# One transfer for the four leftover row blocks of w1, issued earlier, with a new written-out order of all engines

## The chip, the cores and the metric

The kernel runs on one core of a Trainium2 chip. The core has a matmul engine (PE, whose weight loads the profile lists as PEld), a vector engine (DVE), an activation engine (ACT), a small general engine (POOL), a queue engine that mostly issues transfers (SP), and 16 DMA engines that carry them. The metric is the device time of one execution in microseconds (us); lower is better. Three runs of the kernel before gave a median of 148.53 us, 147.5 to 148.92.

## What is computed

The input is a sequence `x` of 2048 rows of 448 numbers. It is normalised row by row, and the normalised rows go two ways: through a diagonal complex recurrence over the sequence (a state-space model), and through a two-layer perceptron with a second normalisation ahead of it. The second result, passed through silu, gates the first.

```python
x = A_x                                   # [1, 2048, 448]
xn = _layernorm(x)
# A: the recurrence; Lam_bar, B_bar from Lambda, log_dt, B; y = 2 Re(C h) + xn * Dskip
h_t = Lam_bar * h_(t-1) + (xn_t @ B_bar.T)
s = 2.0 * real(hs @ C.T) + xn * Dskip
# B: the perceptron, F = 1792
y = _layernorm(xn)
g = silu(gelu(y @ w1 + b1) @ w2 + b2)     # w1 [448, 1792], w2 [1792, 448]
return x + s * g
```

## The kernel before

The sequence is worked in four groups (g = 0 to 3) of 512 positions. For each group the kernel does the first perceptron layer (`mm1_phase`, matmuls on line L661, gelu on ACT at L667 into `gT`), the second layer (`mm2`, L783 and L786, silu at L789 into `g_sb`), the input side of the recurrence (`bu_phase`, L690 into PSUM, copied to `u_sb` and `ue` by `copy` at L301 on ACT or L302 on DVE), the scan itself on DVE (`ssm`: products at L739 to L743, two scans at L749, products at L763 to L768 that make `hx` and `hz`), and the output side (`yt`, L805, L806, L813, L814 on PE, then L826 and L828 on DVE). Matmuls of neighbouring groups are interleaved, so PE changes between the perceptron and the recurrence many times.

The first group is special. Its first layer starts before all of `x` and `w1` has come, so it is done in halves: the first 256 positions (b = 0) for fi = 0 to 11, then fi = 12 and 13 for both halves at 512 columns, then the second 256 positions (b = 1). The names in the code for the transposed normalised rows are `xmT0p0` and `xmT0p1` (first half, transposed on PE) and `xmT1p0`, `xmT1p1` (second half: four DVE instructions at L401 write `xn2_sb`, then a DMA transpose at L77 issued by SP writes `xn2T`).

`w1` has 448 rows, that is three blocks of 128 and a remainder of 64. It is loaded in four parts by columns, of 256, 512, 512 and 512 columns (`CH`, parts 0 to 3). Each part is a transfer of the three full blocks (`w1_c`), a transfer of the remaining 64 rows (`w1r_c`), and a copy on the core of 64 rows into the other half of the partitions (`w1c_c`). A matmul of a part waits for that part's `w1_c` and `w1r_c`, and the second half of each accumulation also for `w1c_c`.

Work is recorded as numbered tasks with the names they read and write. The order in which the tasks are issued is the list `ORDER`, one sequence from which every engine takes its own tasks in turn; `SECOND` lists the tasks that take their second choice of engine (a copy, for example, has ACT first and DVE second). Each engine therefore works in a fixed order, waits where a task needs a name that has not been written yet, and holds everything behind it meanwhile. `D` (the skip weights) and `b2` are one row of 448 each (`dbr0`, `dbr1`), turned into columns by five tiny matmuls on PE (`skip_columns`, L554 and L555) and copied to `db` on DVE.

Of the kernel before, what the change touches and what calls it, by code (L numbers as in the profile page):

```python
# [148 lines left out]
def dram_ap(t, offset, ap):  # L149
    return bass.AP(tensor=t.tensor, offset=offset, ap=ap)  # L150
# [1 line left out]


ORDER = [int(k) for k in """
# [18 lines left out]
""".split()]  # L173
SECOND = [int(k) for k in """
26 29 48 49 59 61 65 69 74 75 76 77 87 89 90 91 113 115 172 178 204 205 206 208 209 210 212 214 216 218 220 222 234 236 238 240 242 244 248 250 252
256 270 277 322 324 336 339 350 352 360 365 399 409 429 443 444 445 446 472 473 475 487 488 528 529 530 542 549 561 575
""".split()]


# [18 lines left out]
def bass_recurrent_scan__ssm_conv_s5__mixer_channel_mlp__prompt_kernel(  # L198
# [11 lines left out]
    L, D, F = 2048, 448, 1792  # L210
# [6 lines left out]
    with ExitStack() as es:  # L217
        def SB(name, shape, dtype=BF):
            return es.enter_context(nc.sbuf_tensor(name, shape, dtype))
# [12 lines left out]
        w1_sb = SB("w1_sb", [128, 4, F])  # L232
# [61 lines left out]
        def act(fn, reads=(), writes=()):  # L294
            kb.add("act", fn, reads, writes)

        def pe(fn, reads=(), writes=(), split=False):
            kb.add("pe", fn, reads, writes, split=split)

        def copy(pairs, rd, wr):  # L300
            kb.either(("act", [lambda e, o=o, i=i: e.activation(o, i, ACT.Copy) for o, i in pairs]),  # L301
                      ("dve", [lambda e, o=o, i=i: e.tensor_copy(o, i) for o, i in pairs]), rd, wr)  # L302

        with nc.Block():  # L304
# [17 lines left out]
            def ld(eng, o, i, writes, reads=()):  # L322
                kb.dma(eng, o, i, reads=reads, writes=writes)
# [4 lines left out]
            def ldx(b0, n, reads=()):  # L328
                ld("sp", x_all[:, b0:b0 + n, :, :], dram_ap(A_x, b0 * 256 * D, [[2 * D, 128], [256 * D, n], [D, 2], [1, D]]),
                   [f"x{b}" for b in range(b0, b0 + n)], reads)  # L330
# [4 lines left out]
            def ldw1(c):  # L335
                a, w = CH[c][0] * 128, CH[c][1] * 128
                ld("sp", w1_sb[:, 0:3, a:a + w], dram_ap(B_w1, a, [[F, 128], [128 * F, 3], [1, w]]), [f"w1_{c}"])
                ld("sp", w1_sb[64:128, 3, a:a + w], dram_ap(B_w1, 384 * F + a, [[F, 64], [1, w]]), [f"w1r_{c}"])
                copy([(w1_sb[0:64, 3, a:a + w], w1_sb[64:128, 2, a:a + w])], [f"w1_{c}"], [f"w1c_{c}"])

            for par in range(2):
                ld("sp", x_all[:, 0, par, :], dram_ap(A_x, par * D, [[2 * D, 128], [1, D]]), [f"x0p{par}"])
            ldx(1, 1)
            ldw1(0)
            ld("act", brows[0:3, :], dram_ap(B_b1, 256, [[512, 3], [1, 512]]), ["br0"], ["br"])
            ld("act", brows[3:4, 0:256], dram_ap(B_b1, 0, [[256, 1], [1, 256]]), ["br1"], ["br"])
            for c in range(1, 4):
                ldw1(c)
# [291 lines left out]
            def fcol(fi):  # L640
                a, n = CH[chunk[fi]]
                return slice(a * 128 + fi - a, (a + n) * 128, n)
# [3 lines left out]
            def wg(g):  # L646
                return f"Wg{g}"

            def mm1_phase(g, b, j, pair, second):
                gx = gb = g % 2  # L650
                cols = slice(0, 512) if b is None else slice(b * 256, (b + 1) * 256)
                rhs = xn2T[:, gx, :, :, :].rearrange("p b (r d) c -> p d (b r) c", r=2) if b is None else xn2T[:, gx, b, :, :].rearrange("p (r d) c -> p d r c", r=2)
                xk2 = [f"xmT{gx}"] if g else ["xmT0p0", "xmT0p1"][:2 * (b != 1)] + ["xmT1p0", "xmT1p1"][:2 * (b != 0)] + ["xmT0"]
                c, bk = chunk[2 * j], MB[pair]

                def dst(bank):
                    return psum[:, bank, cols].rearrange("p (q c) -> p q c", c=128)

                def one_mm(k, n, h):
                    rows, d = slice(64 * h, 64 * h + 64), (0, 1, 2 + h, 3 - h)[n]  # L660
                    return lambda e: e.matmul(dst(bk[k]), w1_sb[rows, d, fcol(2 * j + k)], rhs[rows, d], start=not second and n == 0, stop=second and n == 3)  # L661
                pe([one_mm(h if not second else 1 - h, n, h) for n in range(4 if second else 3) for h in (0, 1)],
                   xk2 + [f"w1_{c}", f"w1r_{c}"] + ([f"w1c_{c}"] if second else []), [f"ps{bk[0]}", f"ps{bk[1]}"], split=True)
                if second:
                    for k in range(2):
                        fi = 2 * j + k
                        act(lambda e, k=k, fi=fi: e.activation(gT[:, gb, fi, cols], psum[:, bk[k], cols], ACT.Gelu_apprx_tanh,  # L667
                                                               bias=b1f[:, fi:fi + 1]),
                            ["b1f", f"ps{bk[k]}", wg(g)], [f"gT{gb}_{fi}_{q}" for q in ((0, 1) if b is None else (b,))])

            def mm1_run(g, b, js, pairs):
                for j in js:
                    mm1_phase(g, b, j, pairs[j - js[0]], False)
                    if j > js[0]:
                        mm1_phase(g, b, j - 1, pairs[j - 1 - js[0]], True)
                mm1_phase(g, b, js[-1], pairs[js[-1] - js[0]], True)
# [294 lines left out]
```

## Time and profile before

| | |
|---|---|
| median of three runs | 148.53 us (147.5 to 148.92) |
| the profiled execution | 148.91 us |
| span of its instructions | 147.2 us |
| what lies around the span | 1.71 us |
| granted PE clock | 0.997 |
| busy | PE 138.9, DVE 129.1, ACT 102.5, POOL 26.0 us |

Busy time of an engine is the time in which it had an instruction under way, and the chain of the profile is followed back from the last instruction, at each step to what released it. In the time lines, the number in brackets behind a row is how long the engine stood idle before it and what released it. `w_sb` stands for `w1_sb` and `w2_sb` alike, `xn_sb` for `xn_sb` and `xn2_sb`, `dk` for the little buffer that first holds the parameter rows, `vs` and `s_w` for the scan's input and output.

### The profile page before, as it was taken

What the parts mean: (1) busy time and instruction counts of PE and PEld (TensorE: products, weight loads), DVE (VectorE), ACT (ScalarE), POOL (GpSimd) and SP (SyncE); (2) the same over time, 40 slices, a digit from 0 to 9 for tenths busy, and PEclk for the clock granted to TensorE, in tenths of its full rate; (3) what the DMA queues carried; (4) which work ended last, traced back from release to release, by engine and by line L of the source; (5) the groups of instructions that cost most, each with busy time, mean ns of one, the idle gap of its engine ahead of it and who ended that gap; (6) DMA issues with size and microseconds to landing.
All of it is one profiled execution on the core that took longest, in us unless ns stands there. A gap on an engine that the chain in (4) does not pass through costs nothing.

```text
span 147.2 us, 3611 instructions
## 1 busy us (share of the span) xinstructions
PE 138.9 (94%) x1454; PEld 92.1 (63%) x1460; DVE 129.1 (88%) x281; ACT 102.5 (70%) x185; POOL 26.0 (18%) x79
## 2 busy tenths in 40 slices
PE   7993999999999999999999999999999999999990
PEld 7882774454455486566758545887766668564870
DVE  2899799999997399999999999596899999999891
ACT  3695899988789986879999931836686996064100
POOL 3484450000960000007600000002000700000000
PEclk9999999999999999999999999999999999999998
DMA  4899992988989946000000627517440011105114
GB/s 111 241 241 130 399 372 74 198 186 114 213 158 165 181 94 130 4 0 2 4 0 0 114 51 143 107 22 141 89 151 0 4 62 62 21 1 107 68 57 125
DMA packets 38850, 15.98 MB, mean 109 GB/s; under 512 B 33193, under 2 KB 38450, under 8 KB 38834
## 3 DMA queue, kind: packets, MB, share of 16 engines
q1 hardware_dynamic: 38276, 15.52, 47.8%
q10 hardware_dynamic: 558, 0.24, 0.6%
q8 instruction: 11, 0.18, 0.5%
q14 instruction: 5, 0.04, 0.1%
HBM read 5.86 MB, written 1.84 MB: 52 GB/s over the span
## 4 chain that ended last, share of the span: by engine, by line
PE 84%; DMA 4%; SPq 4%; DVE 3%; issue 1%; DVEq 0%
PE psum L661 27%; PE psum L783 24%; PE psum L690 15%; PE psum L805 6%; PE psum L806 5%; PE psum L786 4%; DMA w_sb<-in_B_w_dram 4%; SPq L78 4%; PE psum L813 2%; DVE t L828 2%; DVE tmp L826 1%; DVE Bn L861 1%; PE psum L814 0%; DVEq L304 0%; DVEq L131 0%
## 5 line engine op out<-in xcount | busy, mean ns | idle before, releaser
L661 PE MATMUL psum<-xn2T,w_sb 64*128 64x512 bf16 (+1 forms) x476 | 46.9, 340 | 2.6 <-DMA w_sb<-in_B_w_dram 2.3
L667 ACT ACTIVATE gT<-psum,b1f 128x512 bf16<-128x512 f32 (+1 forms) x68 | 37.5, 615 | 6.4 <-PE psum L661 6.1
L783 PE MATMUL psum<-gT,w_sb 128*128 128x512 bf16 x162 | 36.1, 379 | 0.6 <-issue 0.5
L661 PEld LDWEIGHTS psum<-xn2T,w_sb 64*128 64x128 bf16 x476 | 25.2, 109 | 17.9 <-DMA w_sb<-in_B_w_dram 2.5
L783 PEld LDWEIGHTS psum<-gT,w_sb 128*128 128x128 bf16 x168 | 16.2, 98 | 19.1 <-issue 0.4
L690 PE MATMUL psum<-xnT,BT 64*128 64x256 bf16 x392 | 24.6, 270 | 0.0
L690 PEld LDWEIGHTS psum<-xnT,BT 64*128 64x128 bf16 x392 | 18.9, 94 | 6.3 <-issue 0.8
L789 ACT ACTIVATE g_sb<-psum,db 128x512 bf16<-128x512 f32 (+1 forms) x16 | 9.6, 627 | 10.7 <-PE psum L783 8.1
L749 DVE TENSOR_TENSOR_SCAN s_w<-vs,dk 128x786 f32<-128x786 bf16 (+1 forms) x8 | 16.3, 2054 | 0.0
L826 DVE SCALAR_TENSOR_TENSOR tmp<-xnT,db,psum 128x512 f32<-128x512 bf16 (+1 forms) x17 | 10.9, 652 | 2.7 <-PE psum L806 2.2
L301 ACT ACTIVATE vs<-s_w 64x258 bf16<-64x258 f32 (+2 forms) x12 | 8.1, 688 | 6.5 <-DVE s_w L749 6.4
L443 ACT ACTIVATE xn_sb<-x_all,lnw 128x384 bf16<-128x384 bf16 (+2 forms) x18 | 11.0, 649 | 1.0 <-DVE xn_sb L442 0.9
L805 PE MATMUL psum<-hx,CZ 128*128 128x256 bf16 x84 | 10.8, 276 | 0.0
L465 ACT ACT_TABLE_LOAD x8 | 10.3, 1283 | 0.4
L806 PE MATMUL psum<-Bn,CQ 128*128 128x256 bf16 x84 | 10.5, 272 | 0.0
L805 PEld LDWEIGHTS psum<-hx,CZ 128*128 128x128 bf16 x84 | 7.9, 98 | 2.3 <-issue 0.8
L806 PEld LDWEIGHTS psum<-Bn,CQ 128*128 128x128 bf16 x84 | 8.2, 98 | 1.2
L828 DVE TENSOR_TENSOR t<-tmp,g_sb 128x512 bf16<-128x512 f32 (+1 forms) x14 | 8.5, 628 | 0.1
L364 DVE BATCH_NORM_STATS2 lnst<-x_all 128x6 f32<-128x448 bf16 x12 | 7.3, 619 | 0.9 <-DMA x_all<-in_A_x_dram 0.9
L422 POOL TENSOR_SCALAR lnw<-lnmv 128x4 f32<-128x4 f32 x3 | 0.7, 233 | 38.7 <-DVE lnmv L368 38.6
L301 ACT ACTIVATE u_sb<-psum 128x256 bf16<-128x256 f32 (+1 forms) x12 | 5.4, 489 | 2.8 <-PE psum L690 2.8
L761 POOL CAST vs<-cur 128x8 bf16<-128x8 f32 x3 | 2.5, 830 | 26.9 <-DVE cur L759 26.8
(155 smaller groups left out, 190.9 us busy)
## 6 DMA issues: line engine op xcount, KB each, us to landing
x_all<-in_A_x_dram SPq DMA_DIRECT2D x3, 448.0 KB, 6.2
w_sb<-in_B_w_dram SPq DMA_DIRECT2D x3, 448.0 KB, 6.8
out_dram<-Bn SPq DMA_DIRECT2D x6, 224.0 KB, 2.1
w_sb<-in_B_w_dram SPq DMA_DIRECT2D x3, 384.0 KB, 3.9
Bn<-in_A_B_re_dram SPq DMA_DIRECT2D x1, 336.0 KB, 8.1
Bn<-in_A_B_im_dram SPq DMA_DIRECT2D x1, 336.0 KB, 8.5
x_all<-in_A_x_dram SPq DMA_DIRECT2D x2, 112.0 KB, 2.1
x_all<-in_A_x_dram SPq DMA_DIRECT2D x1, 224.0 KB, 2.6
```

The lines of the kernel that those rows point to most:

```text
L301: kb.either(("act", [lambda e, o=o, i=i: e.activation(o, i, ACT.Copy) for o, i in pairs]), ("dve", [lambda e, o=o, i=i: e.tensor_copy(o, i ...
L443: ("act", [lambda e, o=o, i=i: e.activation(o, i, ACT.Identity, bias=nb, scale=rs) for o, i in parts]),
L465: kb.add("act", lambda e: e.preload_act_table_set(what), reads, writes, sem=name)
L661: return lambda e: e.matmul(dst(bk[k]), w1_sb[rows, d, fcol(2 * j + k)], rhs[rows, d], start=not second and n == 0, stop=second and n == 3)
L667: act(lambda e, k=k, fi=fi: e.activation(gT[:, gb, fi, cols], psum[:, bk[k], cols], ACT.Gelu_apprx_tanh, bias=b1f[:, fi:fi + 1]), ["b1f", ...
L690: fns.append(lambda e, rows=rows, bank=bank, m=m, o=o, n=n: e.matmul(psum[:, bank, c * NK:(c + 1) * NK].rearrange("p (b c) -> p b c", b=2) ...
L749: dve(lambda e, so=so, vi=vi, di=di: e.tensor_tensor_scan(so, vi, di, 0.0, ALU.add, ALU.mult), ["v", "vl", "vz", "dk", "dk01"] + ["v3"] * ...
L783: pe([lambda e, fi=fi: e.matmul(psum[:, bk, :], w2_sb[:, fi, 128 * j:128 * j + 128], gT[:, gb, fi, :], start=fi == 0, stop=fi == NF - 1) f ...
L805: pe([lambda e, k=k: e.matmul(par(psum[:, bk, :], 1), CZ[:, k, cols], halves(hx[:, hb, k, 1:NK + 1]), start=k == 0, stop=k == 6) for k in ...
L806: fns = [lambda e, k=k: e.matmul(par(psum[:, bk, :], 0), CQ[:, k, cols], halves(hz[:, hb, k, :]), start=not by_pe and k == 0, stop=not by_ ...
L826: dve([lambda e, o=o, p=p, x=x, d=d: e.scalar_tensor_tensor(out=v(o), in0=x, scalar=d, in1=v(p), op0=ALU.mult, op1=ALU.add) for o, p, x, d ...
L828: dve(lambda e: e.tensor_tensor(t3[:, 512 * j:512 * j + n], s, g_sb[:, hb, 512 * j:512 * j + n], ALU.mult), [ks, f"g{hb}_{j}"], [f"t3{j}"])
```

## The change

The four transfers of the remaining 64 rows become one transfer of all 1792 columns (`w1r`), recorded ahead of part 0 and issued by SP behind the first of the four parts in its order. The row transfers for `D` and `b2` are issued behind the last part of `w1`. Every matmul of the first layer now waits for the one name `w1r`. The copy `w1c_c` still waits for `w1_c`.

```diff
             def ldw1(c):
                 a, w = CH[c][0] * 128, CH[c][1] * 128
                 ld("sp", w1_sb[:, 0:3, a:a + w], dram_ap(B_w1, a, [[F, 128], [128 * F, 3], [1, w]]), [f"w1_{c}"])
-                ld("sp", w1_sb[64:128, 3, a:a + w], dram_ap(B_w1, 384 * F + a, [[F, 64], [1, w]]), [f"w1r_{c}"])
                 copy([(w1_sb[0:64, 3, a:a + w], w1_sb[64:128, 2, a:a + w])], [f"w1_{c}"], [f"w1c_{c}"])
...
             ldx(1, 1)
+            ld("sp", w1_sb[64:128, 3, :], dram_ap(B_w1, 384 * F, [[F, 64], [1, F]]), ["w1r"])
             ldw1(0)
...
-                   xk2 + [f"w1_{c}", f"w1r_{c}"] + ([f"w1c_{c}"] if second else []), [f"ps{bk[0]}", f"ps{bk[1]}"], split=True)
+                   xk2 + [f"w1_{c}", "w1r"] + ([f"w1c_{c}"] if second else []), [f"ps{bk[0]}", f"ps{bk[1]}"], split=True)
...
 ORDER = [int(k) for k in """
-2 3 16 17 14 15 11 9 13 4 44 0 1 22 18 5 24 25 19 20 93 23 94 12 95 45 92 46 42 105 47 96 97 106 49 50 101 107 98 111 110 99 102 48 51 52 100 103 41
+11 12 41 14 15 13 16 17 4 10 18 9 0 1 42 22 89 90 357 91 92 24 19 93 43 44 5 2 46 94 103 102 104 45 105 98 47 95 108 96 23 25 107 106 50 52 99 109 48
...
```

`ORDER` and `SECOND` are replaced as a whole, with three tasks fewer, so tasks move on every engine over the whole program. Three places matter below.

The first is the head of SP's queue, where the difference reads as follows (`w_sb` with 128x3 rows is a part of `w1`, with 64 rows the remainder; `dk<-in_A_Dskip` and `dk<-in_B_b` are the rows of `D` and `b2`; the last row is the transpose of the first group's second half).

```order
 L78 DMA w_sb<-in_B_w_dram 128x3x512
-L78 DMA w_sb<-in_B_w_dram 64x512
+L78 DMA w_sb<-in_B_w_dram 64x1792
 L78 DMA w_sb<-in_B_w_dram 128x3x256
-L78 DMA w_sb<-in_B_w_dram 64x256
+L78 DMA w_sb<-in_B_w_dram 128x3x512 x2
+L78 DMA dk<-in_A_Dskip_dram 1x448
 L78 DMA dk<-in_B_b_dram 1x448
```

Parts 2 and 3 now stand fifth and sixth behind the rows of `x`, with nothing small between them; a transfer of 64 rows of `B_re` that stood between them before has gone far back in the queue.

The second is DVE's stretch up to the second half's normalisation. Before (from the copy of `xn2T` on):

```order
L302 COPY xn2T<-psum 128x512
L401 TENSOR_SCALAR xn_sb<-x_all,lnmv,lnw 128x384
L401 TENSOR_SCALAR xn_sb<-x_all,lnmv,lnw 128x128
L401 TENSOR_SCALAR xn_sb<-x_all,lnmv,lnw 128x384
L401 TENSOR_SCALAR xn_sb<-x_all,lnmv,lnw 128x128
L302 COPY w_sb<-w_sb 64x512
L302 COPY b1f<-psum 128x14
```

and now:

```order
L302 COPY w_sb<-w_sb 64x512
L385 BN_AGGR lnmv<-lnst 128x2 x2
L302 COPY xn2T<-psum 128x512
L486 TENSOR_SCALAR cw<-ang 128x4
L302 COPY b1f<-psum 128x14
L401 TENSOR_SCALAR xn_sb<-x_all,lnmv,lnw 128x384
L401 TENSOR_SCALAR xn_sb<-x_all,lnmv,lnw 128x128
L302 COPY w_sb<-w_sb 64x256
L565 TENSOR_SCALAR s_w<-dk,cw 128x258
L401 TENSOR_SCALAR xn_sb<-x_all,lnmv,lnw 128x384
L401 TENSOR_SCALAR xn_sb<-x_all,lnmv,lnw 128x128
```

Four instructions stand now between the copy of `xn2T` and the last of the four at L401: a small one at L486, the copy of `b1f`, the copy `w1c_0`, which ACT did before, and one at L565. The transpose on SP waits for the last of them.

The third is PE between the second group's output side and the third group's input side (L690 is the input side of the recurrence, L661 the first layer of the last group, L786 the last quarter of the second layer).

```order
+L690 MATMUL psum<-xnT,BT 128x256 x12
 L786 MATMUL psum<-gT,w_sb 64x256 x28
-L690 MATMUL psum<-xnT,BT 128x256 x56
+L690 MATMUL psum<-xnT,BT 128x256 x28
 L661 MATMUL psum<-xn2T,w_sb 128x512 x6
+L690 MATMUL psum<-xnT,BT 128x256 x16
+L661 MATMUL psum<-xn2T,w_sb 128x512 x8
 L690 MATMUL psum<-xnT,BT 128x256 x42
```

The matmuls at L690 ahead of the run of 42 are the same 56, but eight matmuls at L661 of 512 columns have moved ahead of that run, which ends with what DVE copies to `u_sb` for the third group.

More of the change, by code (lines that the diff above doesn't have):

```diff
@@ L154 @@
 ORDER = [int(k) for k in """
[18 rows of a table removed]
[18 rows of a table added]
 """.split()]
 SECOND = [int(k) for k in """
-26 29 48 49 59 61 65 69 74 75 76 77 87 89 90 91 113 115 172 178 204 205 206 208 209 210 212 214 216 218 220 222 234 236 238 240 242 244 248 250 252
-256 270 277 322 324 336 339 350 352 360 365 399 409 429 443 444 445 446 472 473 475 487 488 528 529 530 542 549 561 575
+21 25 27 29 51 56 57 58 59 60 62 66 77 78 80 81 85 88 110 112 169 171 173 176 204 205 207 209 211 213 215 217 219 228 231 233 235 237 239 241 245 251
+253 267 274 275 276 277 321 347 358 361 362 365 404 406 440 441 442 468 469 470 472 484 525 526 528 540 546 558 572
 """.split()]
```

34 rows, old and new, of the table ORDER are left out of this document.

## The prediction

> **What bounds the kernel now.** I read the busy times first, then the chain, then the waits of the engine that the chain names.
>
> ```profile
> PE 138.9 (94%) x1454; PEld 92.1 (63%) x1460; DVE 129.1 (88%) x281; ACT 102.5 (70%) x185; POOL 26.0 (18%) x79
> PE 84%; DMA 4%; SPq 4%; DVE 3%; issue 1%; DVEq 0%
> ```
>
> PE is busy for 94% of the span and makes 84% of the chain, so most of the time can only go if matmuls go, and this change removes none. What is left to win is PE's idle time. The view of PE's waits names its large pieces (total, count, longest):
>
> ```profile
> PE psum L661 <- DMA w_sb<-in_B_w_dram: 2.3, 1, 2.3
> PE psum L377 <- PEq L956: 0.8, 1, 0.8
> PE psum L783 <- issue: 0.5, 3, 0.2
> ```
>
> One wait of 2.3 us stands out, in the first layer of the first group. PE's time line and the chain say where:
>
> ```profile
> 7.43 0.21 PE L554 MATMUL psum<-ident,dk 2*128 2x2 bf16 x3 [0.29 <-DVE xn2T L302]
> 7.69 2.84 PE L661 MATMUL psum<-xn2T,w_sb 64*128 64x256 bf16 x48
> 10.68 0.96 PE L661 MATMUL psum<-xn2T,w_sb 64*128 64x256 bf16 x14 [0.15 <-DVE s_w L565]
> 13.93 7.95 PE L661 MATMUL psum<-xn2T,w_sb 64*128 64x256 bf16 x120 [2.28 <-DMA w_sb<-in_B_w_dram]
> ...
> 7.52 6.31 DMA w_sb<-in_B_w_dram
> 13.93 4.87 PE psum L661 x70
> ```
>
> PE runs 62 matmuls from 7.69 to 11.64 and then stands for 2.28 us. The chain runs through a `w1` transfer issued at 7.52 that lands at 13.83. SP's queue ahead of it:
>
> ```profile
> 0.79 1.36 SPq L78 DMA_DIRECT2D x_all<-in_A_x_dram  x3
> 2.19 2.24 SPq L78 DMA_DIRECT2D w_sb<-in_B_w_dram  x4
> 4.47 0.48 SPq L78 DMA_DIRECT2D dk<-in_B_b_dram  x1
> 5.00 0.23 SPq L78 DMA_DIRECT2D dk<-in_A_Dskip_dram  x1
> 5.27 0.40 SPq L78 DMA_DIRECT2D w_sb<-in_B_w_dram  x1
> 6.25 1.76 SPq L78 DMA_DIRECT2D w_sb<-in_B_w_dram  x3
> 8.38 1.35 SPq L77 DMA_TRANSPOSE xn2T<-xn_sb  x1
> ```
>
> SP needs about half a microsecond for each issue. In the row at 6.25 stand the remainder of part 2, part 3 (at 6.89) and the remainder of part 3 (at 7.52). The table of transfers, asked for single stretches of issue, gives the times to landing of part 2, part 3, its remainder and the transpose:
>
> ```profile
> w_sb<-in_B_w_dram SPq DMA_DIRECT2D x1, 384.0 KB, 3.9
> ...
> w_sb<-in_B_w_dram SPq DMA_DIRECT2D x1, 384.0 KB, 6.8
> w_sb<-in_B_w_dram SPq DMA_DIRECT2D x1, 64.0 KB, 6.3
> xn2T<-xn_sb SPq DMA_TRANSPOSE x1, 6.3
> ```
>
> The same 384 KB took 3.9 us when issued at 5.27 and 6.8 when issued at 6.89. The longer time isn't that of bytes, since a window table (busy share by engine, clock, DMA share, GB/s) shows almost nothing moved while PE waited:
>
> ```profile
> 5.00:6.00 1.00, 1.00 (x13) 1.00 (x11) 1.00 (x3) 0.04 (x1) 0.78 (x4) 1.00 0.96 285
> ...
> 12.00:13.00 1.00, 0.00 (x0) 0.00 (x0) 1.00 (x5) 0.29 (x2) 0.58 (x3) 1.00 0.02 1
> ```
>
> 1 GB/s from 12 to 13 us against 285 earlier: the last pieces of part 3 stood somewhere while little moved. The transpose issued at 8.38 is what joined the same queues after part 3. That it holds part 3 up is my reading and not shown.
>
> [...]
>
> **The change part by part.**
>
> *Part 3 earlier.* Seven issues now stand ahead of it instead of eleven: three of `x`, part 1, the merged remainder, part 0, part 2. By the rows at 0.79 and 2.19 it goes out near 4.5, not at 6.89. With 3.9 us, as part 2 had, it lands near 8.4; with 6.8, its own time before, at 11.3. PE reaches it at 11.64. Both ends are early enough: the 2.28 us go, unless the time is longer than in any row of a `w1` part.
>
> *The first matmul.* The merged remainder (224 KB) stands ahead of part 0, where 64 KB stood: 160 KB more, at 285 GB/s 0.56 us. Part 0 was issued at 3.30 (third in the row at 2.19) and took
>
> ```profile
> w_sb<-in_B_w_dram SPq DMA_DIRECT2D x1, 192.0 KB, 3.5
> ```
>
> so it landed at 6.8 and now lands near 7.4. PE began the first layer at 7.69, after the five tiny matmuls from 7.43 on, which now come 34 matmuls later. So it can begin near 7.43: nothing lost. The ends are 0.26 won and, if the 224 KB move at half that rate, 0.3 lost; I take 0.
>
> *Rows of `D` and `b2`.* They are issued near 5 instead of 4.47, and are needed after 34 matmuls, near 9.6. Even with 3.9 us they are there at 9: hidden, with 0.6 us of cover.
>
> *What is late next: the second half's rows.* The 22 matmuls of the last part on the first half behind, PE needs the transposed rows of the second half. Before, that was at 13.93 + 22 x 4.87/70 = 15.46, and the transpose had landed at 14.7. Without the wait it is at 13.18. The transpose meanwhile goes out later, since DVE has four instructions more ahead of the last one at L401:
>
> ```profile
> 7.24 1.11 DVE L401 TENSOR_SCALAR xn_sb<-x_all,lnmv,lnw 128x384 bf16<-128x384 bf16 x4
> 8.38 0.29 DVE L302 COPY w_sb<-w_sb 64x512 bf16<-64x512 bf16 x1
> 8.59 0.16 DVE L302 COPY b1f<-psum 128x14 f32<-128x14 f32 x1
> 8.79 0.70 DVE L565 TENSOR_SCALAR s_w<-dk,cw 128x258 f32<-128x258 f32 x2
> ```
>
> That is 0.16 for `b1f`, at most 0.29 for `w1c_0` (half the columns of the row shown), 0.35 for one at L565 and 0.16 for L486 (put equal to `b1f`): 0.96, so the issue moves from 8.35 to 9.31. How long it then takes is the open number. The whole run's groups have
>
> ```profile
> xn2T<-xn_sb SPq DMA_TRANSPOSE x4, 4.7
> Cr<-t SPq DMA_TRANSPOSE x6, 3.7
> ```
>
> as medians, and 6.3 for this very one when `w1` was still on its way. With 3.7 it lands at 13.0 and PE waits for nothing; with 4.7 at 14.0 and PE waits 0.8; with 6.3 at 15.6 and PE waits 2.4. Now `w1` should be in by then, so I take the middle of the first two, 13.6: a wait of 0.4. The gain at this point is 2.28 - 0.4 = 1.9.
>
> *ACT.* One at L571 (1.08) now stands ahead of the last six gelus.
>
> ```profile
> 20.71 2.33 ACT L667 ACTIVATE gT<-psum,b1f 128x256 bf16<-128x256 f32 x6 [0.33 <-PE psum L661]
> 22.92 1.08 ACT L571 ACTIVATE s_w<-s_w 128x1032 f32<-128x1032 f32 x1
> ...
> 22.03 9.01 PE psum L783 x41
> ```
>
> The gelus ended at 23.04 before. They now end at 23.04 - 1.9 + 1.08 = 22.2. The second layer starts at 22.03 - 1.9 = 20.1, and its first accumulation takes the `gT` in pieces of 4, 4, 3 and 3 matmuls, the last piece after 11 x 9.01/41 = 2.4 us, at 22.5: hidden, just. If the cover is gone it costs up to 1.08.
>
> *From there to the end.* PE works without a gap, so a gain at 14 us holds until PE meets an engine that didn't get earlier. DVE does, late:
>
> ```profile
> 104.36 0.69 DVE L302 CAST u_sb<-psum 128x512 bf16<-128x512 f32 x1 [0.41 <-PE psum L690]
> 135.78 0.29 DVE L767 TENSOR_TENSOR hx<-pa 128x258 bf16<-128x258 bf16 x1
> 136.13 1.66 PEld L805 LDWEIGHTS psum<-hx,CZ 128*128 128x128 bf16 x14
> ...
> 102.44 2.31 PE psum L690 x42
> 104.75 1.51 PE psum L661 x14
> ```
>
> DVE waits 0.41 us for PE's run of 42 at L690, copies `u_sb` at 104.36, and then works on, with small gaps only, until `hx` at 136.07. PE's weight load at L805 starts 0.06 us after that. So the last third is a chain through DVE as tight as PE's own, which hangs on the end of that run of 42. In the new order eight matmuls at L661 stand ahead of the run; they take 8 x 1.51/14 = 0.86. PE's work is the same in sum, but this chain starts 1.9 - 0.86 = 1.04 earlier rather than 1.9, and PE waits at L805 for the difference. If DVE makes up some of it (its other work around 104 was dealt out anew), the gain lies between 1.04 and 1.9. I take **1.2**, near the lower end, as 0.06 us of slack leave DVE nothing to hide in.
>
> The sum for the profiled execution is 148.91 - 1.2 = 147.7 (its span 147.2, with 1.71 around it). It lies 0.38 above the median, so for the median 148.53 - 1.2 = **147.3**.
>
> **The rivals.**
>
> *The whole gain arrives*: 1.9, or 2.28 with no wait for the second half, and up to 0.3 from the start. For it: PE's 94%. Against it: the 0.06 us at L805. 146.6, down to 145.9.
>
> *Nothing arrives*: the change doesn't do what it says. Part 3 lands at 13.8 whenever it was issued, because something other than its place held it, or the gap comes back at the second half and the DVE chain takes the rest. For it: the stretch at 1 GB/s, whose cause no row names. Against it: the 3.9 of part 2. 148.5, give or take 0.5.
>
> *Slower, by the second half's transpose.* It goes out at 9.31 and takes 6.3 as before: 15.6 against 15.46, so the first gap is moved and not removed, 0.15 lost, and the 0.86 of the new order are lost on top: 149.5. The longest in the table of transfers would make it worse:
>
> ```profile
> Bn<-in_A_B_im_dram SPq DMA_DIRECT2D x1, 336.0 KB, 8.5
> ```
>
> With 8.5 it is 9.31 + 8.5 = 17.8, 2.35 + 0.86 later: 151.7. It decides from a landing at 14.6 (no gain), and costs over 1% from 16.1. For it: the 6.3 that this transpose had, and the same `x` and `w2` transfers behind it. Against it: no `w1` transfer is under way at 9.31 any more.
>
> **How the numbers follow.** The forecast has 0.42 (146.8 to 147.8), the whole gain 0.26, nothing 0.14, the slower case 0.18. About 1% is what a measurement of this kernel can tell from no change: faster means under 147.05, slower over 150.0. Faster is the whole gain, 0.26, and somewhat over a third of the forecast's case, 0.16: 0.42. Slower is two thirds of the last case, 0.12. The rest is 0.46. The range goes from 145.9 (all of the first rival) to 149.1 (the upper end of nothing), and leaves out most of the slower case.
>
> **What would show it.** The profile after should have: SP issuing part 3 near 4.5; no wait of PE at L661 for a `w1` transfer; the transpose issued near 9.3, landing from 13.0 to 14.0; PE waiting at most 0.8 near 13.2 for `xn2T`; the second layer starting near 20.1; DVE's copy of `u_sb` for the third group near 103.3; PE idle up to 0.9 before L805 near 135. The forecast is wrong if the transpose lands after 14.6, if ACT's gelus hold the second layer, if a wait that is new stands between 25 and 100 us, where I have taken the rearranged order to be free, or if DVE's chain is shorter or longer than before.

## The result, and the profile after

The changed kernel took 152.17 us (median of 4 runs, 150.94 to 152.83); the kernel before took 148.01 (4 runs, 147.35 to 148.92). The ratio is 1.028, with a 95% interval of 1.024 to 1.033. The change made the kernel slower by 4.2 us, where the prediction had it faster by 1.2. The profiled execution took 152.83, with a span of 151.1. Ratios leave out single executions that were over 1.5% longer than the fastest of their kernel; the medians here have all of them.

The page's busy line and the line of the granted clock, then the table of PE's waits, of the changed kernel:

```profile
PE 141.9 (94%) x1454; PEld 92.7 (61%) x1460; DVE 129.5 (86%) x279; ACT 102.2 (68%) x186; POOL 28.8 (19%) x80
PEclk9965899999999999999999999999999999999999
...
PE psum L548 <- DMA dk<-in_B_b_dram: 3.4, 1, 3.4
PE psum L377 <- PEq L956: 0.8, 1, 0.8
PE psum L783 <- issue: 0.6, 4, 0.2
```

The wait for part 3 of `w1` is gone, as forecast. In its place stands a longer one, of 3.4 us, at L548. That line and the next hold the six tiny matmuls that turn `b1` into columns, and the first waits for a transfer of `dk`. PE is also busy for 3.0 us more, although it has the same 1454 matmuls, and the line of the clock shows 6, 5 and 8 tenths where before it was 9 in all but the last slice. PE's time line:

```profile
6.20 0.38 PE L406 MATMUL psum<-ident,xn_sb 128*128 128x128 bf16 x4
10.02 0.27 PE L548 MATMUL psum<-ident,dk 4*128 4x3 bf16 x4 [3.44 <-DMA dk<-in_B_b_dram]
10.27 3.81 PE L661 MATMUL psum<-xn2T,w_sb 64*128 64x256 bf16 x34
14.33 10.42 PE L661 MATMUL psum<-xn2T,w_sb 64*128 64x256 bf16 x148
```

The first layer begins at 10.27 instead of 7.69. Its first 34 matmuls take 3.81 us; in the kernel before, 48 of them took 2.84. The window table shows the clock (the column ahead of the last two), of the changed kernel and, below, of the kernel before during its own wait:

```profile
8.00:10.00 2.00, 0.00 (x0) 0.01 (x1) 0.00 (x0) 0.81 (x1) 0.85 (x4) 0.76 0.59 190
10.00:12.00 2.00, 1.99 (x24) 1.47 (x26) 1.56 (x7) 0.00 (x0) 0.00 (x0) 0.50 0.00 0
14.00:16.00 2.00, 2.00 (x25) 1.47 (x25) 1.73 (x9) 1.39 (x5) 1.14 (x3) 0.53 0.81 112
...
12.00:14.00 2.00, 0.07 (x2) 0.10 (x4) 1.86 (x10) 0.60 (x3) 0.58 (x3) 1.00 0.27 57
```

During the new wait the clock falls to one half and stays there until about 16 us. During the old one it did not fall.

What PE waited for is seen in ACT's time line, and its landing in the chain (start, length):

```profile
4.58 0.28 ACT L387 ACTIVATE lnw<-lnmv,eps 128x1 f32<-128x1 f32 x1
4.89 0.23 ACTq L78 DMA_DIRECT2D dk<-in_B_b_dram  x1
...
4.89 4.99 DMA dk<-in_B_b_dram
```

It is the second row transfer of `b1`, of 256 values (`br1`). Before, ACT issued it at once behind the first one, near 2.2. In the new order it stands behind the first two pairs at L387 and L388 and goes out at 4.89. It carries half a kilobyte and takes 4.99 us. The part of `w1` that SP issued just ahead of it (part 3, at 4.46) took 5.4:

```profile
w_sb<-in_B_w_dram SPq DMA_DIRECT2D x1, 384.0 KB, 5.4
```

so part 3 landed at 9.87 and the little row at 9.88. SP's and DVE's time lines show the rest of the pile behind it:

```profile
10.38 0.17 DVE L302 COPY b1f<-psum 128x14 f32<-128x14 f32 x1 [3.11 <-PE psum L549]
12.24 2.11 SPq L77 DMA_TRANSPOSE xn2T<-xn_sb  x1
```

DVE stood behind `b1f`, so the transpose of the second half went out at 12.24 and not at 9.3. PE, being late itself, did not wait for it.

### The profile page after: what moved, and what is told of

Read it like the earlier page. It is cut to its first block, busy times and chain, and to the rows that moved or that the text cites. A ratio compares the mean times of both kernels' runs of the same rounds, so it can differ in the third digit from the quotient of the medians.

```text
span 151.1 us, 3618 instructions
## 1 busy us (share of the span) xinstructions
PE 141.9 (94%) x1454; PEld 92.7 (61%) x1460; DVE 129.5 (86%) x279; ACT 102.2 (68%) x186; POOL 28.8 (19%) x80
## 4 chain that ended last, share of the span: by engine, by line
PE 84%; DVE 5%; DMA 5%; ACT 3%; issue 1%; DVEq 0%; ACTq 0%
PE psum L661 28%; PE psum L783 24%; PE psum L690 13%; PE psum L806 6%; PE psum L805 6%; PE psum L786 4%; DMA dk<-in_B_b_dram 3%; PE psum L813 2%; DMA x_all<-in_A_x_dram 1%; ACT ue L301 1%; DVE Bn L768 1%; DVE pb L764 1%; DVE hx L765 1%; DVE pa L763 1%; DVE Bn L861 1%
## 5 line engine op out<-in xcount | busy, mean ns | idle before, releaser
L661 PE MATMUL psum<-xn2T,w_sb 64*128 64x512 bf16 (+1 forms) x476 | 49.5, 355 | 0.3
L783 PE MATMUL psum<-gT,w_sb 128*128 128x512 bf16 x162 | 36.1, 379 | 0.7 <-issue 0.6
L661 PEld LDWEIGHTS psum<-xn2T,w_sb 64*128 64x128 bf16 x476 | 26.2, 112 | 16.4 <-PE psum L661 1.9
L783 PEld LDWEIGHTS psum<-gT,w_sb 128*128 128x128 bf16 x168 | 16.1, 98 | 19.3 <-issue 0.6
L690 PE MATMUL psum<-xnT,BT 64*128 64x256 bf16 x392 | 25.3, 270 | 0.1
L690 PEld LDWEIGHTS psum<-xnT,BT 64*128 64x128 bf16 x392 | 18.9, 94 | 7.0 <-issue 1.2
L443 ACT ACTIVATE xn_sb<-x_all,lnw 128x448 bf16<-128x448 bf16 (+2 forms) x16 | 10.3, 675 | 1.6 <-DMA xnT<-xn_sb 1.6
L805 PE MATMUL psum<-hx,CZ 128*128 128x256 bf16 x84 | 10.9, 275 | 0.0
L805 PEld LDWEIGHTS psum<-hx,CZ 128*128 128x128 bf16 x84 | 7.9, 98 | 2.7 <-DVE hx L767 0.8
L301 ACT ACTIVATE vs<-s_w 64x258 bf16<-64x258 f32 (+2 forms) x11 | 6.7, 612 | 3.4 <-DVE s_w L749 3.4
L596 DVE SCALAR_TENSOR_TENSOR CQ<-Cr,cw,tmp 128x448 bf16<-128x448 bf16 x7 | 4.6, 673 | 4.0 <-ACT tmp L594 3.9
L301 ACT ACTIVATE ue<-psum 128x512 bf16<-128x512 f32 (+1 forms) x13 | 7.0, 565 | 1.5 <-PE psum L690 1.4
L442 DVE TENSOR_SCALAR xn_sb<-x_all,lnw 128x448 bf16<-128x448 bf16 (+2 forms) x24 | 7.7, 355 | 0.4 <-ACT xn_sb L443 0.2
L422 POOL TENSOR_SCALAR lnw<-lnmv 128x4 f32<-128x4 f32 x3 | 2.2, 743 | 27.1 <-DVE lnmv L368 23.9
```

What stands on the lines that cost most here:

```text
L443: ("act", [lambda e, o=o, i=i: e.activation(o, i, ACT.Identity, bias=nb, scale=rs) for o, i in parts]),
L690: fns.append(lambda e, rows=rows, bank=bank, m=m, o=o, n=n: e.matmul(psum[:, bank, c * NK:(c + 1) * NK].rearrange("p (b c) -> p b c", b=2) ...
L783: pe([lambda e, fi=fi: e.matmul(psum[:, bk, :], w2_sb[:, fi, 128 * j:128 * j + 128], gT[:, gb, fi, :], start=fi == 0, stop=fi == NF - 1) f ...
L805: pe([lambda e, k=k: e.matmul(par(psum[:, bk, :], 1), CZ[:, k, cols], halves(hx[:, hb, k, 1:NK + 1]), start=k == 0, stop=k == 6) for k in ...
```

## The experiments

Theory A: a small row transfer doesn't land before the bulk that was issued ahead of it. With the new order `br1` goes out behind 1568 KB of `w1` (384, 224, 192, 384 and 384), of which nothing has landed by then, so PE stands ahead of its first layer, and then works at half clock. (The expectation of the first run says 1.2 MB, which is too low.) Theory B: the merged remainder and the new order themselves cost the time.

### The row of b1 early

In `ORDER`, 22 and 23 are the two rows of `b1`.

```diff
 ORDER
-42 22 89 90
+42 22 23 89 90
...
-96 23 25 107
+96 25 107
```

> The changed kernel, with the second row transfer of b1 (256 values) moved in ACT's order back to where it stood before, directly behind the first one. Nothing else differs. Theory A (that small transfer, issued at 4.89 behind some 1.2 MB of w1, lands only when they do, at 9.88; PE stands 3.4 us at L548 and then runs the first layer at a lower clock): the row lands near 4.3, the first matmul of the first layer starts near 7.7, the clock stays near 1.0, the second layer starts near 20.5, the time is 147.2 (146.5 to 148). Theory B (what costs is the merged remainder ahead of part 0 and the new order of the engines further on): PE still gets its first rows of w1 late, and the time stays above 150.

Measured: 149.15 us (10 runs, 148.07 to 150.13), ratio to before 1.006, 1.002 to 1.010. Moving this one transfer took 3 of the 4.2 us away. PE's time line:

```profile
6.27 0.18 PE L549 MATMUL psum<-ident,dk 4*128 4x1 bf16 x2
8.83 2.06 PE L661 MATMUL psum<-xn2T,w_sb 64*128 64x256 bf16 x34 [2.38 <-DMA w_sb<-in_B_w_dram]
```

L548 has no wait any more, the clock stays at 1.0 and the 34 matmuls take 2.06. In this execution PE then waited for the merged remainder, which landed near 8.75 (7.1 in the changed kernel). So theory A holds for the larger part, and the forecast 147.2 was still missed by 2: something of theory B is left. The ten executions fall into two groups, four from 148.07 to 148.24 and six from 149.0 on, the profiled one among the six. A remainder that comes late in some of them would explain that; only the one trace shows it.

### The row of b1 late, in the kernel before

The same transfer is moved in the order of the kernel before to the place that it has in the changed one. SP's transfers stay as they were. ACT's order:

```diff
 br0
-br1
 L387 L388 L477 L478 L387 L388
+br1
 L301 xmT0p0
```

> The kernel before, with the second row transfer of b1 moved in ACT's order to the place that it has in the changed kernel (behind the second pair at L387 and L388, issued near 4.9). SP's transfers are as before: what is on its way at 4.9 are part 1, part 0 and their remainders, which landed by 6.91. Theory A: the row lands near 6.9 to 7.0, PE waits 0.2 to 0.5 at L548, the clock stays, 148.2 (147.7 to 148.7). If its place in ACT's queue alone were the cause, it would land 5 us after issue, near 9.9, and the time would be about 151.

Measured: 148.53 (10 runs), ratio 1.001, 0.9985 to 1.0034. PE's waits:

```profile
PE psum L661 <- DMA w_sb<-in_B_w_dram: 1.2, 1, 1.2
...
PE psum L548 <- DMA dk<-in_B_b_dram: 0.2, 1, 0.2
```

Issued at 4.90, as late as in the changed kernel, the row landed at 6.93 and cost 0.2. Its place on ACT alone is not the cause: it took 2.03 us here and 4.99 in the changed kernel, where SP has put parts 2 and 3 ahead of it as well by then.

The first row holds a second lesson. With the same transfers on SP as before, the wait for part 3 is 1.2 here and 2.3 in the execution from which I predicted.

### The wait filled with work

```diff
-                        dummies(5, ["xm0p0"], 1)
+                        dummies(47, ["xm0p0"], 1)
```

> The changed kernel, with 42 more of the matmuls of ones (L377) ahead of the second four transposes on PE, so that PE has work during most of the wait for the row of b1. They compute nothing that is used. The row still lands near 9.9. Theory A with the clock as a part of its own: the granted clock stays near 1.0, the 34 matmuls at L661 take 2.0 us and not 3.8, the second layer starts near 22.3, and the time is some 2.5 us under the changed kernel, 149.5 (149 to 150.2). If the low clock comes from something else than the idle time, the 34 matmuls keep their 3.8 us and the time stays at 152.

Measured: 150.68 (4 runs, 150.43 to 150.91), ratio 1.0145, 1.0118 to 1.0172.

```profile
5.79 3.49 PE L377 MATMUL psum<-const-bfloat16-1.0 128*128 128x128 bf16 x50
10.28 0.27 PE L548 MATMUL psum<-ident,dk 4*128 4x3 bf16 x4 [0.78 <-DMA dk<-in_B_b_dram]
10.53 2.18 PE L661 MATMUL psum<-xn2T,w_sb 64*128 64x256 bf16 x34
```

The row is as late as before, but the clock stays at 1.0 and the 34 matmuls take 2.18 instead of 3.81. The second layer starts at 22.99 rather than 24.90. So 1.9 us of the slowdown in the profiled execution were the clock, which fell because PE stood idle. (The matmuls that fill it made the first layer start 0.3 later, so 1.9 is net of that.) In the medians the filled kernel is 1.5 below the changed one, whose four executions differ in the clock: their mean clocks were 0.977, 0.977, 0.982 and 0.989, their times 152.83, 152.71, 151.63 and 150.94. The forecast of 149.5 was 1.2 too low, mostly for a reason that the table below shows.

### The change alone, in the old order

Only what the change says, in the order of the kernel before: `w1r` in place of `w1r_1`, the three others left out, `dbr0` and `dbr1` behind `w1_3` on SP. `br1` stays early. SP's order:

```diff
 w1_1
-w1r_1
+w1r
 w1_0
-w1r_0
-dbr1 dbr0
 w1_2 Bn60
-w1r_2
 w1_3
-w1r_3
+dbr0 dbr1
```

> The kernel before in its own order on all engines, with only what the change says: one transfer of the remainder in place of that of part 1, none for the other parts, and the rows of D and b2 behind the last part on SP. The row of b1 stays early. Theory A, taken for every small row behind bulk: the rows of D and b2 land with the last part, near 10.2, and as PE's order has L554 ahead of the first layer, PE stands near 2.7 us there and its clock falls: 151 (149.5 to 152.5). If only the row on ACT's queue is affected, D and b2 land within 3 us of their issue, near 8.5, PE stands 1 us, keeps its clock, and the time is 147 (146.3 to 147.7).

Measured: 152.26 (4 runs), ratio 1.025, 1.021 to 1.028. The wait, the chain's row for the transfer, and the first matmuls:

```profile
PE psum L554 <- DMA dk<-in_B_b_dram: 3.9, 1, 3.9
...
6.06 4.57 DMA dk<-in_B_b_dram
...
11.06 5.15 PE L661 MATMUL psum<-xn2T,w_sb 64*128 64x256 bf16 x48
```

Here the rows of `D` and `b2` are the small ones behind the bulk. The later one lands at 10.63, PE stands for 3.9 us, and the clock falls (48 matmuls in 5.15). The new order avoids this by putting L554 behind 34 matmuls. It loses the same by another row.

### The rows moved alone

The kernel before with its four remainders, and only `dbr0` and `dbr1` behind the last of them. SP's order:

```diff
 w1_1 w1r_1 w1_0 w1r_0
-dbr1 dbr0
 w1_2 Bn60 w1r_2 w1_3 w1r_3
+dbr1 dbr0
```

> The kernel before with its four separate remainders, and only the rows of D and b2 moved on SP behind the last of them. Theory A: they are issued near 7.2 and land with part 3, near 11 to 13.8, so PE, whose next task is L554, stands from 7.2 to about 12.5 before the first layer begins, its clock falls by half for some microseconds after, and the time is 155 (153 to 158). If small rows are not held by bulk, they land 2.5 us after issue, near 9.8, PE stands 2.6 us, no longer waits later for part 3, and the time is about that of before, 148 to 149.

Measured: 153.56 (one run), where the kernel before had a median of 147.80 beside it.

```profile
PE psum L554 <- DMA dk<-in_A_Dskip_dram: 5.1, 1, 5.1
...
8.00 3.71 DMA dk<-in_A_Dskip_dram
```

The rows land at 11.7, 0.4 behind the last remainder. Moving the rows costs 5.8 us by itself in this one run, so it is no saving at all where PE needs them ahead of its first layer.

### The merge alone

`w1r` in place of `w1r_1`, the others left out, the rows where they were. SP's order:

```diff
 w1_1
-w1r_1
+w1r
 w1_0
-w1r_0
 dbr1 dbr0 w1_2 Bn60
-w1r_2
 w1_3
-w1r_3
```

> The kernel before in its own order, with one transfer of the remainder (224 KB) in place of that of part 1 and none for the other parts. The rows of D and b2 stay where they were, ahead of parts 2 and 3, and that of b1 stays early. Theory A (a small row lands with the bulk that was issued ahead of it): D and b2, issued near 4.1, land with part 0, near 7.7; PE waits 0.3 to 0.5 at L554 and the clock stays; part 3 goes out near 5.4 and lands near 10.5, so the wait of 2.3 us is gone; the second layer starts near 20.1, and with the old order of the engines behind it (125.2 us from there to the end) the time is 146.6 (146 to 147.3), faster than before by 1%. If the merged transfer itself costs (part 0 late by over 2 us), it is 148 or more.

Measured: 147.61 (10 runs, 147.24 to 149.35), ratio 1.0015, 0.9978 to 1.0052. The forecast of 146.6 was missed: no gain is seen.

```profile
8.03 0.21 PE L554 MATMUL psum<-ident,dk 2*128 2x2 bf16 x3 [1.45 <-DMA dk<-in_A_Dskip_dram]
8.17 0.19 PE L555 MATMUL psum<-ident,dk 2*64 2x2 bf16 x2
8.29 4.46 PE L661 MATMUL psum<-xn2T,w_sb 64*128 64x256 bf16 x48
```

The rows of `D` and `b2` land with part 0 now, at 7.7 and 7.9. Part 0 stands behind the merged remainder; in the changed kernel, where SP's queue begins alike, it landed at 7.63, and in the kernel before at 6.75. In this execution the clock fell with a wait of 1.45. By the window table it fell near 8.5, just after PE had begun again:

```profile
6.00:8.00 2.00, 0.58 (x12) 0.39 (x9) 1.71 (x9) 1.16 (x5) 1.30 (x7) 1.00 1.10 278
8.00:10.00 2.00, 1.97 (x23) 1.51 (x25) 1.87 (x9) 1.38 (x2) 1.53 (x8) 0.62 0.92 256
10.00:12.00 2.00, 2.00 (x24) 1.41 (x20) 1.93 (x8) 0.84 (x2) 1.83 (x3) 0.53 1.18 142
```

Four of the ten executions had a mean clock of 0.988 and took 148.8 to 149.4; the six others had 0.993 to 1.0 and took 147.2 to 147.7.

### The merge alone, with that wait filled

The same, with:

```diff
-                        dummies(5, ["xm0p0"], 1)
+                        dummies(27, ["xm0p0"], 1)
```

> The kernel that only merges the remainders (D and b2 ahead of parts 2 and 3), with 22 more matmuls of ones ahead of the second four transposes, so that PE has work during most of the 1.45 us for which it stood at L554. That kernel had executions at a granted clock of 0.988 and about 148.8 us, and others at 0.993 to 1.0 and about 147.4. If the idle 1.45 us ahead of the first layer makes the lower clock, all executions are at 0.993 or more here and between 147.0 and 147.9, though the matmuls add nothing. If the lower clock comes and goes for a reason of its own, a third or so of them still lie near 148.8.

Measured: 147.74 (10 runs, 147.21 to 148.42), ratio 0.999, 0.996 to 1.0015. All ten had a clock of 0.994 or more, and the 48 matmuls took 2.85 in the profiled one:

```profile
8.86 2.85 PE L661 MATMUL psum<-xn2T,w_sb 64*128 64x256 bf16 x48
```

The executions near 148.8 are gone, as they should be if idle time ahead of the first layer makes the lower clock. Four in ten against none in ten would not show it alone, since the kernel before also had a mean clock under 0.99 in 6 of its 55 executions beside these runs. For the wait of 3.44 it is shown: there the mean clock was under 0.99 in four of four executions, and at 0.996 or more in four of four with the wait filled. For the wait of 1.45 it is likely. As the filling ends later than the rows land, the median doesn't fall. The spread to 148.4 was not expected, and no clock explains it.

### All small rows early, in the old order and in the new

```diff
-                ld("sp", drows[i:i + 1, :], ...
+                ld("act", drows[i:i + 1, :], ...
```

`dbr0` and `dbr1` stand directly behind `br0` and `br1` on ACT's queue, and all four go out by 3.1. In the old order:

> As the one that only merges the remainders, but D and b2 are issued by ACT's queue near 2.5, directly behind the rows of b1, ahead of nearly all the bulk. Theory A: they land by 5, PE has no wait at L554; the first layer starts when part 0 is there, near 7.7; part 3 lands near 10; the second layer starts near 20.0, and the time is 146.4 (145.8 to 147.2). If it is SP's order and not the bulk that makes small rows late, this one differs from the merged one by less than 0.2 as well, but then D and b2 land late there without part 0 landing late.

Measured: 147.18 (8 runs, 146.91 to 147.48), ratio 0.9956, 0.9938 to 0.9974. It is under both kernels, by 0.4% and clear of the noise against the kernel before, but 0.8 above its forecast. Part 3, forecast to land near 10, was issued at 5.01 and landed at 12.09, just ahead of PE's need. In the order of the changed kernel:

> The changed kernel with its new order, all small rows early: the second row of b1 directly behind the first, D and b2 behind that on ACT's queue. Against the last one it differs in the order of the engines alone. The three runs of the new order so far have 126.1 to 126.2 us from the start of the second layer to the end, the three of the old one 125.1 to 125.2. If that 1.0 belongs to the order, this kernel takes 147.5 (146.8 to 148.5), 1.0 more than the old order with the same transfers. If it came from being early or late against transfers, the two are equal within 0.4.

Measured: 148.09 (10 runs, 147.43 to 150.41), ratio 1.001, 0.997 to 1.004. With the rows early in both, the new order takes 0.8 more in the median of the executions that the ratios keep (147.95 and 147.18), and 0.4 in the two profiled ones. The start of the second layer, of the old order and then the new, and the weight load of the last L805, in the same order:

```profile
20.28 9.24 PE L783 MATMUL psum<-gT,w_sb 128*128 128x512 bf16 x42
134.61 1.66 PEld L805 LDWEIGHTS psum<-hx,CZ 128*128 128x128 bf16 x14
...
19.76 9.24 PE L783 MATMUL psum<-gT,w_sb 128*128 128x512 bf16 x42
135.24 1.46 PEld L805 LDWEIGHTS psum<-hx,CZ 128*128 128x128 bf16 x14 [0.51 <-DVE hx L767]
```

The new order reaches the second layer 0.5 earlier and the last L805 0.6 later. The same sum holds for every kernel so far:

| | second layer starts | span | from there to the end |
|---|---|---|---|
| old order: before | 22.03 | 147.2 | 125.2 |
| row of b1 late | 21.24 | 146.4 | 125.2 |
| change alone | 25.41 | 150.5 | 125.1 |
| merge alone | 21.71 | 147.1 | 125.4 |
| merge, wait filled | 21.01 | 146.2 | 125.2 |
| rows alone | 26.39 | 151.8 | 125.4 |
| merge, rows early | 20.28 | 145.7 | 125.4 |
| new order: changed | 24.90 | 151.1 | 126.2 |
| row of b1 early | 21.11 | 147.2 | 126.1 |
| wait filled | 22.99 | 149.2 | 126.2 |
| rows early | 19.76 | 146.1 | 126.3 |

The time of each is its start, up to the second layer, and a constant: 125.1 to 125.4 in the old order, 126.1 to 126.3 in the new.

### The eight matmuls at L661 moved back

The new order with all rows early, and the eight matmuls of L661 that the prediction priced at 0.86 put back behind the run of 42 at L690, with their gelu. PE's order:

```diff
 L661 x6
-L690 x16
-L661 x8
-L690 x42
-L661 x28
+L690 x58
+L661 x36
```

> The changed kernel's order with all small rows early, as in the last run of that order, and with the eight matmuls at L661 (and their gelu) moved back behind the run of 42 at L690 that makes u_sb for the third group. The prediction's step: the chain through DVE starts 0.86 earlier, and as it ends where PE waits at L805, the time falls by 0.6 to 0.9, to 147.3. The rival: the 1.0 us of the new order is made of many small waits of PE, of which this is none, since PE reaches L805 hardly earlier than DVE: the time stays within 0.3 of 148.1.

Measured: 149.80 (4 runs, 149.71 to 149.92), ratio 1.013, 1.009 to 1.016: neither. DVE's time line:

```profile
103.83 0.69 DVE L302 CAST u_sb<-psum 128x512 bf16<-128x512 f32 x1 [1.48 <-PE psum L690]
106.83 0.96 DVE L740 TENSOR_TENSOR pb<-u_sb,WT 128x1536 bf16<-128x1536 bf16 x1 [2.31 <-ACT u_sb L301]
```

DVE's next step now waits 2.31 us for ACT's copies of `u_sb`, where it waited 0.23 in the kernel before. The edit made a new wait of its own, so it tells nothing of the 0.86. The two traces with all rows early still tell where the 1.0 us of the new order arises. DVE's copy of `u_sb` for the third group and the end of `hx`, of the old order and then the new:

```profile
102.84 0.69 DVE L302 CAST u_sb<-psum 128x512 bf16<-128x512 f32 x1 [0.41 <-PE psum L690]
134.26 0.29 DVE L767 TENSOR_TENSOR hx<-pa 128x258 bf16<-128x258 bf16 x1
...
103.56 0.69 DVE L302 CAST u_sb<-psum 128x512 bf16<-128x512 f32 x1 [1.67 <-PE psum L690]
134.89 0.29 DVE L767 TENSOR_TENSOR hx<-pa 128x258 bf16<-128x258 bf16 x1
```

From the start of the second layer to that copy the old order takes 82.56 and the new one 83.80, 1.24 more. From the copy to the end of `hx` they take 31.7 and 31.6. In the eleven kernels of the table the first stretch is 82.3 to 82.6 in the old order and 83.6 to 83.8 in the new, and the second 31.7 and 31.6. So DVE's chain is late at its start, where the prediction looked, and makes up 0.1 at most. Of the matmuls recorded in the first stretch, only those at L661 differ in number, 202 and 210. These are the eight, at the prediction's price 0.86 of the 1.24. No run moved them without making a new wait, so this share is worked out and not measured.

PE, however, is late by itself: from the start of the second layer to its last run at L783 it takes 108.50 in the old order (20.28 to 128.78) and 109.26 in the new (19.76 to 129.02). It then waits only 0.18 for `hx` at L805. Had DVE's chain alone been earlier, these 0.18 were what could be won. What makes PE itself 0.76 slower on the way stays open.

## Why the prediction was wrong

**The wait for part 3: right in kind.** Part 3 went out at 4.46 (forecast 4.5) and landed at 9.87 (forecast 8.4 to 11.3). With every small row early the second layer starts at 19.76, 2.27 ahead of the kernel before, which is the 2.28 that the sum took away. Its size was that of one execution, however. The execution from which I worked, 148.91, was near the top of the runs, and the kernel with the same transfers on SP had a wait of 1.2 at a time of 148.1. So that 2.27 and 2.28 agree so closely is luck in part. What held part 3 for 6.8 us in the kernel before stays open. The prediction's reading, the transpose issued behind it, isn't borne out: with the merge alone, the change alone and the rows alone the transpose also went out while part 3 was on its way (at 8.3 to 8.6), and part 3 took 4.6, 5.4 and 4.8. With the merge and the rows early in the old order it took 7.1. Two counts were off, and nothing hangs on them: twelve issues stood ahead of part 3 before, not eleven, and parts 2 and 3 now stand fourth and fifth behind the rows of `x`, not fifth and sixth.

**The first matmul: this step failed.** The prediction said that the first layer can begin near 7.43, "nothing lost", with bounds of 0.26 won and 0.3 lost. It began at 10.27. I reckoned only with part 0 and with L554. L548, which stands ahead of the first layer as well, needs `br1`, and the new order had moved `br1` on ACT's queue from the second place among the rows of `b1` to behind six instructions. The prediction spoke of SP's queue alone, and so did the three places named ahead of it. Late issue by itself would have cost 0.2 (the row late in the old order); late issue behind parts 2 and 3 cost 3.44. Against the kernel with the rows early (first matmul at 7.55, second layer at 19.76) the changed kernel's first matmul is 2.7 later, by the wait, and its second layer 5.1 later. Of the other 2.4, 2.2 are the clock: with the wait filled, the stretch from the first matmul of the first layer to the second layer falls from 14.63 to 12.46, against 12.21 with the rows early. Nor was the rest of the step safe: with `br1` early and the others late, the first layer began at 8.83, as the merged remainder took 6.1 in that execution.

**The rows of D and b2: wrong as priced, hidden all the same.** I took 3.9 us at the most, the time of part 2, for their landing at 9. Issued at that place they landed at 10.1 and 10.2 in the changed kernel. PE reached L554 at 14.02, so they cost nothing there. In the old order the same rows cost 3.9 us and the clock.

**The clock: not in the prediction at all.** The granted clock of 0.997 stands in the table, and the prediction's own window row has 1.00 during the wait of 2.28, but no wait was priced with a lower clock.

**The second half's transpose and ACT's gelus: without effect.** The transpose went out at 12.24 (forecast 9.3) as DVE stood behind `b1f`, and landed at 15.66, but PE was late itself and had no wait for it. The rival on the slow side, with 149.5 to 151.7, came nearest to the measured time, but by luck: its cause, PE waiting for the transpose, didn't occur. The second layer waited for no `gT`.

**From there to the end: right in size, and partly by luck.** The prediction took 0 to 0.86 off the gain for the new order and used 0.7. The traces show 0.9 to 1.0 from the second layer to the end. DVE's chain starts late by 1.2, as it said in kind. But PE's wait for `hx` at L805, by which that was to cost time, is only 0.18; the other 0.76 are PE's own and were not forecast.

So the sum of the mended terms, with the row of `b1` late, is: 2.3 gained, 5.1 lost by `br1`, 1.0 lost by the order, 3.8 more than before, against 3.9 measured between the two spans. The terms come from profiled executions of the same kernels, so the sum shows only that nothing large is left out.

Theory A, taken to the letter, is too strict. With `b1` late in the old order the row issued at 4.90 landed at 6.93, and part 0, issued ahead of it, at 7.09. With `b1` early in the new order the rows of `D` and `b2`, issued by SP behind part 3, landed at 9.96 and 10.14, and part 3 at 11.20. No row of `b1`, `D` or `b2` in any trace landed more than 0.4 us after the last bulk transfer issued ahead of it, but some landed over 1 us before it: the second row of `b1` in the kernel before at 4.45, with part 1 at 6.04, and the rows of `D` and `b2` named above. So a row can land as late as the bulk queued ahead of it, and can also land before the last of it.

In the changed kernel the row issued on ACT's queue at 4.89 landed at 9.88, within 0.01 us of part 3 on SP's queue. What held the row there is not shown.

## What to carry to other kernels

When a transfer is put ahead of others, list every small transfer that is issued after it and needed before it, on all queues, and count each as landing with the bulk ahead of it, unless a trace shows it earlier: the row of `b1` took 4.99 us here behind parts 2 and 3, and 2.03 without them. Small rows that something early needs go out first. An idle wait of PE early in a kernel is to be priced with the slower matmuls that can follow it (after the wait of 3.44 us 34 of them took 3.81 us, and 2.18 with the wait filled), and a wait taken from one profiled execution is to be checked against the spread of the runs before it is counted as the gain.

## What the runs showed of the hardware

A row of half a kilobyte took 4.99 us behind bulk transfers, and 2.03 us when issued at the same time behind less. It was late on either queue: in the changed kernel the rows of `D` and `b2`, issued by SP at 4.99 and 5.42, took 5.1 and 4.8.

Idle PE time does not lower the clock by its length alone. Waits of 3.44, 3.9 and 5.1 us ahead of the first layer brought it to 0.50. With the merge alone (1.45 us in its trace) it fell in some executions and not in others. Yet 2.38 us (the row of `b1` early) and 2.28 us (before, inside the first layer) left it at 1.0 in their traces. Nor does the low clock last as long as the wait. By the clock that the traces record it stood at one half from 9.05 to 15.88 in the changed kernel, from 9.10 to 15.93 with the change alone and from 10.82 to 17.64 with the rows alone, 6.83 us each time, and from 8.47 to 11.89, half of that, with the merge alone. What sets the moment of the fall, and the length of the low clock, is not shown.
